# Moving a kernel's operand transposes from TensorE to the DMA queue, with a two-step issue order and a new order of the first chunks

## The chip, the cores and the metric

One core of one Trainium2 chip. The metric is the device time of one execution in microseconds (us). A span in a profile is shorter than the device time of the same execution, mostly by 1.7 to 1.8 us.

The granted clock is the clock that TensorE got, as a share of full speed (1.00). The DMA share is the mean busy share of the core's 16 DMA engines, by the time that packets took.

Engines: PE is TensorE's matmul side, PEld its weight load, DVE VectorE, ACT ScalarE, POOL GpSimd, SP SyncE; "SPq" is SP's sequencer. In the traces it issues all loads, stores and DMA transposes of this kernel, one after another (in that of before 99.47 us for 0.36 us, 99.88 for 0.43, 100.40 for 0.65).

## The reference, cut to what matters

```python
def _attn_ref(q, k, v, alpha):                 # (4, 8, 768, 48) each
    for t in range(S):
        state = alpha[:, :, t, :, None] * state + einsum('bhd,bhe->bhde', k[:, :, t], v[:, :, t])
        y[:, :, t] = einsum('bhd,bhde->bhe', q[:, :, t], state)

def _moe_ref(x, w_in, w_out):                  # x (3072, 384), w_in (384, 2048), w_out (2048, 384)
    h = x @ w_in
    return (h * np.cos(h)) @ w_out
```

A gated linear attention with a recurrent state, followed by a feed-forward layer with a cosine gate. The kernel works through the 3072 tokens in 24 chunks of 128.

## The kernel before

Each chunk passes through units that are named by a letter. An order string says in which order the units of all chunks are recorded, and the traces show the engines running their shares in that order: in that of the changed kernel TensorE does F, S, A, G, V, Y, C from 82.07 to 87.87 us and SP v, a, D, k, k, a, D, e, v, e from 69.50 to 82.79 us, as in its string below. The program has no other scheduler. The units that matter here:

```python
    def operands(j, qeng):            # "o": k and q scaled, in bf16, on GpSimd
        nc.gpsimd.tensor_tensor(out=khb[:, j % 3, :, 0:D], in0=k_sb, in1=icp..., op=ALU.mult)
        qeng.tensor_tensor(out=qhb[:, j % 3, :, 0:D], in0=q_sb, in1=cp..., op=ALU.mult)
        # [cut: v cast, decay of the state]

    def transposes(j):                # "T": eight 128x128 transposes on TensorE, into PSUM
        t = ps.tile([C, 2 * NP * C], BF, tag="g")
        for i, src in enumerate((khb, qhb)):
            for p in range(NP):
                nc.tensor.transpose(t[...], src[:, j % 3, 2 * p : 2 * p + 2]..., ident_bf)

    def ev_transposes(j):             # "t": VectorE copies them to SBUF
        t = work.tile([C, 2 * NP * C], BF, tag="qkT", bufs=3)
        nc.vector.tensor_copy(out=t, in_=qkT_ps.pop(j))

    # "A" scores: 8 matmuls on qkT; "m" mask; "S" state, "u" its update; "Y" outputs, "y" their copy
    # "F","G": halves of ff1, 24 matmuls each; "f","g": cosine on ScalarE; "p","q": gate on VectorE
    # "V","W": halves of ff2, 8 matmuls each; "e": result to SBUF and its store, issued by SP
    # "a","k","v": loads (k stands for k and q); "l","C","E": logarithm, cumulative sum, exponential
    # "w": warm-up matmuls on zeros

    START = ("a0 v0 z0 k0 20 N0 i0 v1 a2 w20 w20 w6 c0 d0 O0 a1 a3 w9 S0 u0 T0 t0 ... "
             "F0 E1 11 21 G0 k3 u1 o2 T2 f0 m1 g0 t2 p0 Y1 y1 A2 ...")        # [cut]
    run(START)
    for s in range(S0, NCH + 2):      # one chunk per step; S0 = 4
        g = (s + 3) // 2
        odd = s % 2 == 1
        V = s - 2 if s - 2 > 1 else -1
        run(f"a{s + 7} k{s + 4} v{s + 4}")
        run(f"o{s + 2} T{s + 1} t{s + 1} F{s} f{s} S{s + 1} u{s + 1} A{s + 1} m{s + 1}")
        run(f"V{V} G{s} g{s} p{s} Y{s + 1} y{s + 1} q{s}")
        if odd:
            run(f"N{g} l{g + 1}")
        run(f"W{V} e{V}")
        if odd:
            run(f"C{g} E{g}")
```

## Time and profile before

| | before |
|---|---|
| device time, median | 208.5 us (207.56 to 209.18, 4 runs) |
| profiled span | 208.2 us |
| PE busy | 196.8 us, 95% |
| PE busy from 70 to 170 us | 100.00 of 100.00 us |
| DMA share from 70 to 170 us | 0.66 |
| chain per two chunks | 14.76 us |

The page's line of busy time, and the lines, from its costliest groups, for the mask that evicts the scores and for the PSUM copy of the transposes. Columns of a group: line, engine, operation, output<-input, shape, count; then busy us and mean ns of one; then the engine's idle time just before.

```profile
PE 196.8 (95%) x2645; PEld 149.0 (72%) x2647; DVE 136.7 (66%) x163; ACT 130.4 (63%) x142; POOL 79.6 (38%) x124
...
L236 DVE TENSOR_TENSOR t<-t,mask_f 128x1024 bf16<-128x1024 f32 x24 | 29.2, 1215 | 0.0
...
L216 DVE COPY t<-t 128x1024 bf16<-128x1024 bf16 x24 | 16.5, 687 | 8.1 <-PE t L210 8.1
```

The table of windows of before. Columns: window in us, its length, busy time of PE, PEld, DVE, ACT and POOL (instructions started), granted TensorE clock, DMA share, GB/s.

```profile
32.00:34.00 2.00, 1.89 (x23) 1.62 (x20) 2.00 (x3) 0.62 (x1) 0.00 (x0) 0.50 0.98 363
...
70.00:170.00 100.00, 100.00 (x1474) 79.89 (x1472) 70.13 (x83) 68.19 (x75) 45.38 (x68) 1.00 0.66 134
```

In the steady part PE is never idle, and VectorE, ScalarE and GpSimd are each busy 71% of the time or less.

The chain of waits of before, in order of time (start us, length us, what). It is PE and nothing else. One period of two chunks runs from one cumulative sum to the next; the pieces on line 210 are the eight transposes of a chunk.

```profile
68.56 0.18 PE cum_new L161
68.74 0.08 PE cum_new L165 x4
68.82 0.47 PE t L210 x8
69.29 1.34 PE t L323 x24
...
75.96 0.45 PE t L210 x8
...
83.32 0.18 PE cum_new L161
```

From 68.56 to 83.32 us is 14.76 us, and 0.47 + 0.45 = 0.92 us of it are transposes. The loop's first ff1 starts at 54.75 us and the last piece of the chain, the last ScalarE copy, at 204.40 us, so the loop takes 149.65 us between these two marks.

### The profile page before, as it was taken

To read this page: it belongs to the slowest core of one execution; us is meant where nothing else is said; L and a number is where in the kernel's file an instruction comes from. 1 tells how busy PE (TensorE), PEld (TensorE's weight loads), DVE (VectorE), ACT (ScalarE), POOL (GpSimd) and SP (SyncE) were. 2 spreads that over 40 slices of the span, in tenths; PEclk is the share of its full clock that TensorE was granted. 3 is DMA by queue.
4 is the path that set the end of the run, shared out by engine and by line. 5 is a ranking of instruction groups with operands and counts; after the bars stand their busy time and mean duration, and the time that the engine had idled before them with its cause. 6 is when DMAs were issued, how large, how long until landed. Compare 5 with 4: busy or idle time off the path is not lost.

```text
span 208.2 us, 6187 instructions
## 1 busy us (share of the span) xinstructions
PE 196.8 (95%) x2645; PEld 149.0 (72%) x2647; DVE 136.7 (66%) x163; ACT 130.4 (63%) x142; POOL 79.6 (38%) x124
## 2 busy tenths in 40 slices
PE   7996869899999999999999999999999999999982
PEld 2343558677787887877878787787878878787851
DVE  7106857799776668487686685766776776777320
ACT  2064594998964955955937839739659558434420
POOL 3005362485570371561730931912804617401000
PEclk9999997999999999999999999999999999999999
DMA  6999999999999377566765955874774461101112
GB/s 139 312 197 319 186 218 360 260 179 199 179 225 191 80 151 157 113 148 123 160 131 93 188 117 106 162 152 97 135 154 94 100 114 43 41 2 39 38 38 77
DMA packets 106204, 30.29 MB, mean 145 GB/s; under 512 B 100288, under 2 KB 105408, under 8 KB 106176
## 3 DMA queue, kind: packets, MB, share of 16 engines
q1 hardware_dynamic: 106176, 29.89, 66.6%
q8 instruction: 20, 0.33, 0.7%
q14 instruction: 8, 0.07, 0.1%
HBM read 25.17 MB, written 4.72 MB: 144 GB/s over the span
## 4 chain that ended last, share of the span: by engine, by line
PE 82%; DVE 6%; DMA 4%; issue 4%; POOL 1%; SPq 1%; ACT 0%; POOLq 0%; DVEq 0%; ACTq 0%
PE o_new L347 32%; PE t L323 29%; PE t L304 8%; PE t L210 5%; DMA t<-in_k_dram 4%; PE t L227 3%; PE t L249 2%; PE cum_new L161 1%; DVE w_114 L121 1%; DVE g_new L338 1%; DVE t L216 1%; DVE qhb L193 1%; PE cum_new L165 1%; DVE t L309 1%; DVE t L236 1%
## 5 line engine op out<-in xcount | busy, mean ns | idle before, releaser
L331 ACT ACTIVATE c_sb<-t,halfpi 128x1024 bf16<-128x1024 f32 x48 | 53.3, 1115 | 41.7 <-PE t L323 41.3
L323 PE MATMUL t<-t,w_114 128*128 128x128 bf16 x1152 | 72.6, 220 | 0.4 <-DVE g_new L338 0.4
L347 PE MATMUL o_new<-w_116,g_new 128*128 128x384 bf16 x384 | 70.2, 327 | 0.6 <-ACT o_sb L363 0.6
L323 PEld LDWEIGHTS <-w_114 128*128 128x128 bf16 x1152 | 67.9, 99 | 3.5 <-issue 0.5
L338 DVE TENSOR_TENSOR g_new<-t,c_sb 128x1024 bf16<-128x1024 f32 x48 | 58.4, 1219 | 15.2 <-ACT c_sb L331 14.7
L191 POOL TENSOR_TENSOR khb<-t,icp_new 128x384 bf16<-128x384 f32 x24 | 25.0, 1041 | 74.8 <-ACT icp_new L179 73.7
L347 PEld LDWEIGHTS <-g_new 128*128 128x128 bf16 x384 | 34.1, 98 | 24.2 <-issue 0.8
L263 POOL TENSOR_TENSOR ub<-sc,Em 128x384 bf16<-128x384 f32 x20 | 17.4, 870 | 33.1 <-DVE sc L261 33.1
L236 DVE TENSOR_TENSOR t<-t,mask_f 128x1024 bf16<-128x1024 f32 x24 | 29.2, 1215 | 0.0
L193 POOL TENSOR_TENSOR qhb<-t,cp_new 128x384 bf16<-128x384 f32 x22 | 22.0, 1000 | 0.0
L216 DVE COPY t<-t 128x1024 bf16<-128x1024 bf16 x24 | 16.5, 687 | 8.1 <-PE t L210 8.1
L309 DVE CAST t<-t 128x384 bf16<-128x384 f32 x24 | 13.3, 554 | 11.4 <-PE t L304 11.3
L363 ACT ACTIVATE o_sb<-o_new 128x384 f32<-128x384 f32 x22 | 10.7, 485 | 15.9 <-PE o_new L347 15.8
L261 DVE TENSOR_TENSOR sc<-t,ub 128x384 f32<-128x384 f32 x20 | 11.1, 557 | 13.8 <-PE t L249 13.8
L370 PE MATMUL w_ps<-warm 128*128 128x512 bf16 x61 | 17.3, 435 | 1.4 <-DVE warm L56 1.2
L331 ACT ACT_TABLE_LOAD x13 | 16.7, 1283 | 0.2
L141 ACT ACT_TABLE_LOAD x13 | 16.7, 1283 | 0.2
L304 PE MATMUL t<-t,vpb 128*64 128x128 bf16 x288 | 15.9, 222 | 0.2 <-DVE t L216 0.2
L179 ACT ACTIVATE icp_new<-cum_new 128x768 f32<-128x768 f32 (+1 forms) x13 | 9.8, 757 | 7.3 <-PE cum_new L165 7.3
L370 PEld LDWEIGHTS <-warm 128*128 128x128 bf16 x63 | 6.5, 109 | 10.4 <-issue 4.5
L304 PE MATMUL t<-t,ub 128*64 128x128 bf16 x160 | 13.0, 227 | 1.0 <-DVE t L216 0.8
L304 PEld LDWEIGHTS <-vpb 128*64 128x64 bf16 x288 | 13.1, 111 | 0.9 <-issue 0.4
(47 smaller groups left out, 152.9 us busy)
## 6 DMA issues: line engine op xcount, KB each, us to landing
a_new<-in_alpha_dram SPq DMA_DIRECT2D x24, 192.0 KB, 3.7
t<-in_v_dram SPq DMA_DIRECT2D x24, 192.0 KB, 4.3
t<-in_k_dram SPq DMA_DIRECT2D x24, 192.0 KB, 4.0
t<-in_q_dram SPq DMA_DIRECT2D x24, 192.0 KB, 4.3
out_dram<-o_sb SPq DMA_DIRECT2D x24, 192.0 KB, 2.0
w1f<-in_moe_w_in_dram SPq DMA_DIRECT2D x2, 1536.0 KB, 7.8
w2f<-in_moe_w_out_dram SPq DMA_DIRECT2D x2, 1536.0 KB, 10.3
```

Of the source, the lines that this page charges most:

```text
L141: nc.scalar.preload_act_table_set("natural_log_exp_and_others")
L191: nc.gpsimd.tensor_tensor(out=khb[:, j % 3, :, 0:D], in0=k_sb, in1=icp.rearrange("s (h d) -> s h d", h=H), op=ALU.mult)
L193: qeng.tensor_tensor(out=qhb[:, j % 3, :, 0:D], in0=q_sb, in1=cp[:, 0:HD].rearrange("s (h d) -> s h d", h=H), op=ALU.mult)
L216: nc.vector.tensor_copy(out=t, in_=qkT_ps.pop(j))
L236: nc.vector.tensor_tensor(out=t.rearrange("s (h t) -> s h t", h=H), in0=A_ps.pop(j).rearrange("s (h t) -> s h t", h=H), in1=mask_f.unsquee ...
L263: eng.tensor_tensor(out=ub[:, j % 3, :, 0:96].rearrange("r p (a e) -> r p a e", a=2), in0=sc.rearrange("r p (a e) -> r p a e", a=2), in1=E ...
L304: nc.tensor.matmul(t[64 * half : 64 * half + 64, kt * C : (kt + 1) * C], lhsT, rhs, start=start, stop=stop, skip_group_check=True)
L323: nc.tensor.matmul(t[:, f], w1[:, kk, ft * C : (ft + 1) * C], x_t[j][:, kk], start=(kk == 0), stop=(kk == 2))
L331: nc.scalar.activation(out=c_sb, in_=h_ps[j, half], func=AF.Sin, bias=halfpi, scale=1.0)
L338: nc.vector.tensor_tensor(out=g_t[j][:, half * HF : (half + 1) * HF], in0=h_ps.pop((j, half)), in1=c_t.pop((j, half)), op=ALU.mult)
L347: nc.tensor.matmul(o_ps[j][:, 0:DM], g_t[j][:, ft], w2[:, ft], start=(f == 0 and (half == 0 or not whole)), stop=(f == HF - 1 and (half == ...
L370: nc.tensor.matmul(w_ps, warm[:, 0:C], warm, start=True, stop=True)
```

## The change

Its intent: from chunk 8 on, the eight transposes leave TensorE and become one DMA transpose (unit "D"), SBUF to SBUF, of 128x1024 bf16 elements. k and q share one tile so that one DMA does both. The loop now records two chunks per step, in an order that was searched in a timing model and that places each D, each load and each store. The order of the first chunks was searched likewise.

```diff
+    JT = 8
-    qhb = consts.tile([C, 3, H, 64], BF, tag="qhb")
-    khb = consts.tile([C, 3, H, 64], BF, tag="khb")
+    kqb = consts.tile([C, 3, 2, H, 64], BF, tag="kqb")
     [cut: the same renaming where they are written and read]
+    def dma_transposes(j):
+        t = work.tile([C, 2 * NP * C], BF, tag="qkT", bufs=3)
+        nc.sync.dma_start_transpose(t.rearrange("r (p s) -> r p s", s=C),
+                                    kqb[:, j % 3].rearrange("s i h d -> s (i h d)"))
+        qkT_t[j] = t
     START = (
-        "a0 v0 z0 k0 20 N0 i0 v1 a2 w20 w20 w6 c0 d0 O0 a1 a3 w9 S0 u0 T0 t0 i1 k1 z1 c1 10 d1 k2 "
+        "v0 a0 k2 k0 a1 i1 a2 a4 a3 i0 w20 w20 w7 c0 d0 O0 w7 T0 z0 t0 S0 k1 10 c1 d1 l1 u0 v1 "
     [cut: the rest of both strings]
-    for s in range(S0, NCH + 2):     [cut: the loop of before, shown above]
+    STEPS = (
+        "T1 t1 o2 v4 F0 S1 A1 a8 m1 f0 o3 u1 G0 p0 D2 g0 V-2 Y1 C2 k4 k5 E2 y1 W-2 T2 a9 q0 F1 "
+        "N2 D3 e-2 t2 S2 A2 V-1 m2 l3 f1 u2 v5 G1 g1 Y2 p1 y2 W-1 q1 e-1 "
+    )
+    for s in range(4, NCH + 2, 2):
+        for u in STEPS.split():
+            n = int(u[1:]) + (s // 2 if u[0] in "NlCE" else s)
+            if not (u[0] in "VWe" and n < 2 or u[0] in "Tt" and n >= JT or u[0] == "D" and n < JT):
+                run(f"{u[0]}{n}")
```

In the names of a double step, D2 and D3 transpose chunks s+2 and s+3. A2 reads the first in the same double step, A1 of the next reads the second.

## The prediction

> **What bounds the kernel now.** From about 54 us on, TensorE alone. The page gives PE 95% busy, granted clock 0.99; the table of 10 us windows shows PE 10.00 of 10.00 from 60 to 190 us, with DVE, ACT and POOL below 9. The chain of waits is nothing but PE pieces from 54 to 198 us. Two chunks take 14.76 us (the cumulative sums stand at 68.56, 83.32 and 98.08 us). Each chunk's eight transposes are 0.45 to 0.47 us of that chain. Before 54 us the DMA share is about 1.0, PE's first useful matmul comes at 14.4 us, and the chain passes through loads, casts, operands and PSUM copies.
>
> **What the change does.** For chunks 8 to 23 the 8 PE transposes and DVE's PSUM copy (687 ns each) go: 16 x 0.46 = 7.4 us of PE and 11 us of DVE. Only the PE part lies on the chain. In their place come 16 DMA transposes of 256 KB (SBUF to SBUF) on SP's queue, which also carries the loads.
> [...] From 80 to 170 us the DMA share is 0.65, about 9.6 us per two chunks[...]. Issue on SP: loads take 0.4 to 0.8 us each, about 6 us per two chunks. [...]
> Latency: D2 is issued about 3 us into a double step, two loads ahead of it, and its scores come 4 us later. D3 stands behind five loads, but is read 7 us later. I expect both to land in time, the first with little slack.
> The two-step order keeps PE's amount of work; a PE that never waits gains nothing from it.
> The first-chunks order gives up the early first weight load (11th transfer, not third), takes the weight cast out of ACT's way ahead of the first logarithm, and runs both first ff1 halves before the second weight half is needed. Adding loads up at 1 us each and 4.5 us per weight half (estimates from the GB/s row), PE can be kept busy from about 30 us; the opening ends at 50 to 54 us against 54.3. I count 2 us.
>
> **On the critical path.** 7.4 us (steady) + 2 us (opening) - 0.5 us (late transposes) = about 9 us. Predicted 199.5 us (ratio 0.957), 196 to 204.5 for 8 in 10. Faster by over 2%: 0.80; within 2%: 0.12; slower by over 2%: 0.08.
>
> **What would show it.** PE at 10.00 of 10.00 from 70 to 180 us; 13.8 to 13.9 us per two chunks; transposes landing 2 to 5 us after issue; DMA share 0.75 to 0.9 in the steady part; the loop's first ff1 at 51 to 54 us. Wrong would be: scores waiting for the transposed tile, loads late at POOL, or SP's issues closing up without gaps.
>
> **What would make it wrong.** A DMA transpose that takes more of the engines than its bytes say[...]; an issue on SP of over 4 us; loads queued ahead of a transpose making it late each step; or an opening in which the later weights cost more than the earlier operands give.

The sum of the critical path: 7.4 + 2 - 0.5 is 8.9, about 9 us, and 208.5 - 9 is 199.5 us. The 0.5 us in it is worked out from no trace. The 0.4 to 0.8 us for a load's issue are the usual ones: in the trace of before, from 60 to 172 us, it took 0.65 us in the median, 0.39 to 2.15 us in all, and SP's issues came to 5.0 to 7.7 us per two chunks. The 4 us of issue that would make it wrong is an estimate from the 6 and 13.8 us: two of them would fill what is left.

## More of the kernel before

The profiled execution is one draw among the runs: that of before took 209.99 us, more than any of the four timed ones.

## The result, and the profile after

| | before | after |
|---|---|---|
| device time, median | 208.5 us (4 runs) | 202.9 us (202.03 to 203.05, 4 runs) |
| ratio | | 0.9726 (95% interval 0.9679 to 0.9772) |
| profiled span | 208.2 us | 200.3 us |
| chain per two chunks | 14.76 us | 13.87 us |
| loop, first ff1 to last copy | 149.65 us | 142.50 us |
| DMA share from 70 to 170 us | 0.66 | 1.04 |

A ratio is the mean time of one kernel's fast runs over that of the other's of the same rounds, so it is not quite the ratio of the medians quoted.

The same two windows of the changed kernel:

```profile
32.00:34.00 2.00, 2.00 (x39) 2.00 (x37) 0.73 (x2) 1.79 (x3) 0.00 (x0) 1.00 1.11 338
...
70.00:170.00 100.00, 100.00 (x1456) 77.89 (x1451) 66.71 (x73) 72.22 (x78) 46.99 (x71) 1.00 1.04 176
```

One period of its chain of waits, where no piece of the transposes' line is left:

```profile
73.63 0.27 PE cum_new L161
...
74.24 1.32 PE o_new L353 x8
75.56 1.34 PE t L329 x24
76.90 0.17 PE t L255 x4
77.07 0.33 PE t L233 x8
...
87.50 0.27 PE cum_new L161
```

And the transposes in its table of DMA issues (count, then median us from issue to landing):

```profile
t<-kqb SPq DMA_TRANSPOSE x16, 4.1
```

87.50 - 73.63 is 13.87 us. The chain goes on without a break: PE is still at 100.00 of 100.00 us, and no score matmul (line 233) waits for a DMA anywhere in the run. The first ff1 of the loop starts at 53.83 us and the last copy at 196.33 us, 142.50 us: 7.15 us less than before. The profile shows 7.9 us of gain, the timed runs only 5.6. The experiments had to explain that difference, and what each of the three parts of the change contributes.

### The profile page after: what moved, and what is told of

The parts are those of the page before. It is cut to its first block, busy times and chain, and to the rows that moved or that the text cites. A ratio compares the mean times of both kernels' runs of the same rounds, so it can differ in the third digit from the quotient of the medians.

```text
span 200.3 us, 5940 instructions
## 1 busy us (share of the span) xinstructions
PE 190.6 (95%) x2535; PEld 141.0 (70%) x2535; DVE 126.0 (63%) x146; ACT 126.5 (63%) x139; POOL 78.1 (39%) x124
## 3 DMA queue, kind: packets, MB, share of 16 engines
q1 hardware_dynamic: 123072, 34.09, 90.8%
## 4 chain that ended last, share of the span: by engine, by line
PE 82%; DVE 7%; issue 5%; DMA 2%; SPq 1%; POOL 1%; ACT 0%; POOLq 0%; DVEq 0%; ACTq 0%
PE t L329 31%; PE o_new L353 31%; PE t L310 7%; PE t L233 3%; DMA t<-in_k_dram 2%; DVE g_new L344 2%; PE t L210 2%; PE cum_new L161 2%; PE w_ps L376 2%; PE t L255 2%; DVE t L242 1%; DVE t L216 1%; DVE t L315 1%; PE cum_new L165 1%; SPq L105 1%
## 5 line engine op out<-in xcount | busy, mean ns | idle before, releaser
L329 PE MATMUL t<-t,w 128*128 128x128 bf16 x1152 | 72.0, 219 | 0.9 <-DVE t L315 0.7
L329 PEld LDWEIGHTS <-w 128*128 128x128 bf16 x1152 | 67.0, 98 | 6.1 <-DVE t L315 0.8
L353 PE MATMUL o_new<-w,g_new 128*128 128x384 bf16 x384 | 69.9, 326 | 0.7 <-ACT o_sb L369 0.6
L191 POOL TENSOR_TENSOR kqb<-t,icp_new 128x384 bf16<-128x384 f32 x24 | 24.2, 1010 | 27.3 <-ACT icp_new L179 14.8
L193 POOL TENSOR_TENSOR kqb<-t,cp_new 128x384 bf16<-128x384 f32 x22 | 22.0, 1000 | 1.8 <-DMA t<-in_q_dram 1.8
L376 PE MATMUL w_ps<-warm 128*128 128x512 bf16 x79 | 20.4, 408 | 1.3 <-DVE warm L58 1.2
L195 POOL CAST vpb<-t 128x384 bf16<-128x384 f32 x24 | 12.5, 520 | 19.6 <-DMA t<-in_v_dram 12.7
L148 ACT ACTIVATE lnab<-a_new 128x768 bf16<-128x768 f32 (+1 forms) x13 | 10.2, 798 | 10.3 <-DMA a_new<-in_alpha_dram 8.2
L376 PEld LDWEIGHTS <-warm 128*128 128x128 bf16 x79 | 7.7, 104 | 10.9 <-issue 3.1
L310 PE MATMUL t<-t,ub 128*64 128x128 bf16 x160 | 12.9, 225 | 0.9 <-DVE t L216 0.8
L310 PEld LDWEIGHTS <-ub 128*64 128x64 bf16 x160 | 9.8, 109 | 5.4 <-issue 2.9
```

The source lines that it names most:

```text
L191: nc.gpsimd.tensor_tensor(out=kqb[:, j % 3, 0, :, 0:D], in0=k_sb, in1=icp.rearrange("s (h d) -> s h d", h=H), op=ALU.mult)
L193: qeng.tensor_tensor(out=kqb[:, j % 3, 1, :, 0:D], in0=q_sb, in1=cp[:, 0:HD].rearrange("s (h d) -> s h d", h=H), op=ALU.mult)
L310: nc.tensor.matmul(t[64 * half : 64 * half + 64, kt * C : (kt + 1) * C], lhsT, rhs, start=start, stop=stop, skip_group_check=True)
L329: nc.tensor.matmul(t[:, f], w1[:, kk, ft * C : (ft + 1) * C], x_t[j][:, kk], start=(kk == 0), stop=(kk == 2))
L353: nc.tensor.matmul(o_ps[j][:, 0:DM], g_t[j][:, ft], w2[:, ft], start=(f == 0 and (half == 0 or not whole)), stop=(f == HF - 1 and (half == ...
L376: nc.tensor.matmul(w_ps, warm[:, 0:C], warm, start=True, stop=True)
```

## The experiments

Eleven runs in three batches, each batch on one chip together with the kernel before. Where a later text says "the loop", it means the stretch from its first ff1 to the last copy.

| run | what it is | median us | ratio to before |
|---|---|---|---|
| e0_after, e10_after | the changed kernel again | 202.92, 202.2 | 0.972, 0.9687 |
| e1_no_dma | both new orders, all transposes on TensorE | 209.45 | 1.0051 |
| e2_old_start | the changed loop, the old first-chunks order | 202.64 | 0.9705 |
| e3_dma_only | DMA transposes in the old orders, behind the step's loads | 208.78 | 1.0035 |
| e4_dma_late | the same, in the step that reads them | 330.17 | 1.5798 |
| e5_dma_first | as e3, but ahead of the step's loads | 204.03 | 0.975 |
| e6_start_warm | as e2, with 7 more warm-up matmuls | 201.58 | 0.9646 |
| e7_from6 | as e6, DMA transposes from chunk 6 | 204.45 | 0.9785 |
| e8_from7 | as e6, DMA transposes from chunk 7 | 202.02 | 0.9675 |
| e9_twice | as e6, every DMA transpose issued twice | 210.06 | 1.0058 |

### The changed kernel again (e0_after)

No edit.

> The changed kernel once more, as it is, so that the parts can be compared with it on the same chip. Both theories: 202 to 203.5 us, ratio to the kernel before 0.969 to 0.977.

202.92 us, ratio 0.972: the first measurement holds. The profile of this run, with a clock of 1.0, has these two marks, the loop's first ff1 and the last copy:

```profile
54.86 1.34 PE t L329 x24
...
197.36 0.49 ACT o_sb L369
```

The loop is 142.50 us again, but it starts at 54.86 us, 1.03 us later than in the first profile of the changed kernel (53.83), and no earlier than in that of before (54.75).

### The two orders without the DMA transposes (e1_no_dma)

```diff
-    JT = 8
+    JT = 24
```

> The changed kernel with all 24 chunks transposed on TensorE: the two new orders alone, no DMA transpose. Theory (only the 16 chunks' transposes on TensorE's chain are worth anything in the steady part): 7.0 to 7.4 us longer than the changed kernel, so 209.5 to 210.5 us, ratio to before about 1.007. Rival (the two-step order is what gains, by ending waits): at most 2 us longer, 203 to 205 us. Period per two chunks: theory 14.76 us.

209.45 us, ratio 1.0051 (interval 1.0017 to 1.0086), 6.5 us longer than the changed kernel. The theory asked for 7.0 to 7.4 us: the medians fall 0.5 us short of that, while the interval covers the ratio given, 1.007. The rival (at most 2 us) fell. The chain of waits of this run has these two marks, the loop's first ff1 (21 of its 24 matmuls lie in the queried window) and the last copy:

```profile
53.85 1.17 PE t L329 x21
...
203.50 0.49 ACT o_sb L369
```

203.50 - 53.85 is 149.65 us, the loop of before to the hundredth. So for a TensorE that never waits the two-step order is worth nothing in the loop. The two new orders together made the kernel slower, by the mean about 1 us, and with equal loops that can only be the opening.

### The old order of the first chunks (e2_old_start)

```diff
     START = (
-        "v0 a0 k2 k0 a1 i1 a2 a4 a3 i0 w20 w20 w7 c0 d0 O0 w7 T0 z0 t0 S0 k1 10 c1 d1 l1 u0 v1 "
+        "a0 v0 z0 k0 20 N0 i0 v1 a2 w20 w20 w6 c0 d0 O0 a1 a3 w9 S0 u0 T0 t0 i1 k1 z1 c1 10 d1 k2 "
     [cut: the whole string of before, with a11 added at its end]
```

> The changed kernel's loop and DMA transposes behind the first-chunks order of the kernel before. The measured gain is 5.6 us, and the loop alone shows 7.0 us in the two traces. Theory (the new first-chunks order costs over a us in most runs, and the profiled run of before was a slow draw): 200.5 to 202 us, at least 1 us shorter than the changed kernel. Rival (the new first-chunks order is worth its 1 to 2 us, as the two traces show): 204 us or more, at least 1 us longer.

202.64 us (201.11 to 202.72), 0.3 us shorter than the changed kernel in the same batch. Neither side is met: the new opening brings nothing, but it doesn't cost over 1 us either, in the median. The single runs tell more. The old opening has more than one kind of run. With a granted clock of 1.0 this kernel's span was 199.2 us (one run), with 0.989 to 0.996 it was 200.5 to 200.9. The kernel before shows the like over the three batches: 10 of its 33 runs had a clock of 0.999 or more and spans of 205.7 to 206.2 us, 23 had 0.99 to 0.992 and 206.9 to 208.3 us, 1.4 us more by the means. Like compared with like in this batch, the spans of this run are 6.5 us (lower clock) and 6.8 us (full clock) shorter than those of before, near the loop's 7.15. The window of before from 32 to 34 us, shown above, is the fall of the clock: 0.50. The window of this run's table for the same time:

```profile
32.00:34.00 2.00, 1.89 (x23) 1.62 (x20) 2.00 (x3) 0.49 (x1) 0.00 (x0) 0.50 1.05 385
```

The windows of before give 0.72 from 30 to 32 us, 0.50 to 34 us, 0.85 to 35 us and 1.00 after that. Ahead of the fall, from 28 to 30 us, TensorE was busy for 0.81 of 2.00 us at a clock of 1.00, and the longest gap between matmuls that the trace shows from 14 to 36 us was 0.78 us. What brings the fall on, and why some runs of one kernel have it and others not, these windows don't show.

The two profiles show 7.9 us where the timed runs show 5.6, because they are draws from opposite ends. The profiled execution of before took 1.5 us more than the median of its timed runs (209.99 against 208.5), that of the changed kernel 0.9 us less (202.03 against 202.9). The fall of the clock alone doesn't explain this. Most timed runs of before have the lower clock too, and they form two groups themselves: 17 with spans of 206.9 to 207.5 us and 6 with 208.0 to 208.3, where the profile stands. And in the changed kernel's sixteen runs it is the longer ones that have the full clock: 201.0 to 201.3 us at 1.0, 199.9 to 200.6 at 0.995 to 0.999. What else differs between runs was not found.

The new opening mostly avoids the fall (0.995 or more in all sixteen runs of the changed kernel), yet ends no earlier: the loop starts at 54.86 us in e0_after and at 54.67 in e10_after. The chain of waits of the changed kernel's first profile has warm-up matmuls on it, 4.2 us in all. That of before has none. The new order string has 79 of them, the old one 63:

```profile
17.94 1.75 PE w_ps L376 x8
...
20.62 1.19 PE w_ps L376 x5
...
22.26 1.29 PE w_ps L376 x6
```

Just before the loop it passes through DVE:

```profile
49.28 0.56 DVE o_sb L367
...
50.36 1.21 DVE t L242
51.57 1.13 DVE g_new L344
52.70 0.47 DVE t L315
```

Yet TensorE is busy for 3.41 of the 3.90 us from 49.3 to 53.2 us there, so in that stretch these evictions hold it up for no more than about 0.5 us. Neither the warm-up matmuls nor the evictions were tested by a run of their own. Why the new opening ends no earlier stays open.

### The DMA transposes alone (e3_dma_only)

```diff
-        run(f"o{s + 2} T{s + 1} t{s + 1} F{s} f{s} S{s + 1} u{s + 1} A{s + 1} m{s + 1}")
+        T = f"T{s + 1} t{s + 1}" if s + 1 < JT else ""
+        DT = f"D{s + 2}" if s + 2 >= JT else ""
+        run(f"o{s + 2} {DT} {T} F{s} f{s} S{s + 1} u{s + 1} A{s + 1} m{s + 1}")
```

> The kernel before, both its orders kept, with the DMA transposes alone: issued right behind each chunk's operands, one step ahead of the scores, after that step's four loads. Theory (a TensorE that never waits gains nothing from the two-step order, and one step is lead enough): 7.0 to 7.4 us shorter than before, 201 to 202 us, ratio 0.965 to 0.968, period 13.8 to 13.9 us per two chunks. Rival (the two-step pattern is needed to bring the transposes in time past the loads): scores wait each step, ratio above 0.98.

208.78 us, ratio 1.0035 (0.9995 to 1.0074). My theory fell: with the same 7.2 us of work taken off TensorE, nothing was gained. The waits of this run (engine, line, what it waited for; total us, times, longest):

```profile
PEld L233 <- DMA t<-kqb: 5.6, 8, 1.2
...
PE t L233 <- DMA t<-kqb: 4.4, 6, 1.1
```

Half of the 16 chunks' score matmuls now wait for their transposed tile. (The expectations of the next two runs add these two lines up, to 14 times and to 10 us. That was a mistake: weight load and matmul wait for the same tile, so it is at least 5.6 us and 8 times.) SP's issues in one step show where the time goes. Columns: start us, us of the issue, what.

```profile
84.82 0.36 SPq L371 DMA_DIRECT2D out_dram<-o_sb  x1
85.22 0.43 SPq L100 DMA_DIRECT2D a_new<-in_alpha_dram  x1
85.70 0.67 SPq L105 DMA_DIRECT2D t<-in_k_dram  x1
86.42 1.90 SPq L105 DMA_DIRECT2D t<-in_q_dram  x1
88.37 0.78 SPq L110 DMA_DIRECT2D t<-in_v_dram  x1
89.31 1.48 SPq L221 DMA_TRANSPOSE t<-kqb  x1
```

The transpose goes out 4.5 us after the store that opened the step, and lands 3.8 us (the run's median) after that, in the next step, when the scores want it. From the first cumulative sum in that stretch to the eighth the seven periods take 14.78 us each, against 14.70 before. The 16 chunks are eight periods, so the counted waits are 0.7 us per period, of the 0.98 that separate 14.78 from the 13.80 of the changed kernel (the mean of six of its periods); the rest I did not follow.

### The transpose in the step that reads it (e4_dma_late)

```diff
-        run(f"o{s + 2} T{s + 1} t{s + 1} F{s} f{s} S{s + 1} u{s + 1} A{s + 1} m{s + 1}")
+        T = f"T{s + 1} t{s + 1}" if s + 1 < JT else f"D{s + 1}"
+        run(f"o{s + 2} {T} F{s} f{s} S{s + 1} u{s + 1} A{s + 1} m{s + 1}")
```

> The kernel before with both its orders; the DMA transpose stands exactly where the eight TensorE transposes stood, in the step that reads it (no lead at all, and one step earlier in the operands' life). Theory (what decides is when the transpose lands against the scores of its chunk, and in the run with one step of lead it came about 0.6 us too late 14 times of 16): with the operands ready a whole step earlier the transpose waits only for SP, which reaches it after a store and four loads, about 4 us into the step; it lands 4 us later while TensorE wants it about 1.5 us into the step: each step waits 5 to 6 us, 16 x 5.5 less 7.2 gives about +80 us, 280 to 295 us. Rival (latency is not what held the one-step version back, but the 16 DMA engines or SP's issue time are full): about the same as the one-step version, 208 to 212 us, since bytes and issues are the same.

330.17 us. The rival fell: with the same bytes and the same issues the kernel is 121 us slower, so it is the landing time that decides. My number was too small twice over. The waits are longer than 5.5 us:

```profile
PEld L233 <- DMA t<-kqb: 97.2, 16, 7.4
```

And in the stretches with these waits the granted clock is lower: 0.84, 0.60 and 0.74 in the three windows from 150 to 180 us, 0.83 in the mean of the run, against 0.992 in e3. A window of its table:

```profile
160.00:170.00 10.00, 7.46 (x68) 5.24 (x69) 3.42 (x4) 1.11 (x1) 1.75 (x4) 0.60 0.26 42
```

An ff1 half at 165.61 us, shortly after a wait of 7.20 us, takes 2.60 us; the next one, at 170.14 us, takes 1.50. 16 waits make 97 us, which leaves 31 us between 330 and (202 + 97) us. The pages of the runs show most of it: the same 2519 PE instructions kept PE busy for 219.0 us here and for 191.3 us in e3, 27.7 us more, at a mean clock of 0.83 against 0.992.

### The transpose ahead of the loads (e5_dma_first)

```diff
-        run(f"a{s + 7} k{s + 4} v{s + 4}")
-        run(f"o{s + 2} {DT} {T} F{s} ...")
+        run(f"o{s + 2} {DT} a{s + 7} k{s + 4} v{s + 4}")
+        run(f"{T} F{s} ...")
```

> The kernel before with both its orders and one-step lead as in the run that gained nothing, but each transpose is issued ahead of that step's four loads instead of behind them. Theory (the transpose's place in SP's queue decides, not the two-step order): it goes out about 3 us earlier, waits of scores for the transposed tile fall from 10 us to under 2, and the time is 201.5 to 203.5 us, ratio 0.966 to 0.975. Rival (only the two-step order hides it, or the DMA engines are full): ratio above 0.985.

204.03 us (202.23 to 204.69), ratio 0.975. One unit moved past four loads in one queue turns 208.78 into 204.03 us, with both orders of before otherwise kept. The waits:

```profile
PEld L233 <- DMA t<-kqb: 0.5, 1, 0.5
PE t L233 <- DMA t<-kqb: 0.4, 1, 0.4
```

SP's issues in one of its steps:

```profile
100.23 1.24 SPq L221 DMA_TRANSPOSE t<-kqb  x1
101.51 0.57 SPq L100 DMA_DIRECT2D a_new<-in_alpha_dram  x1
102.14 0.62 SPq L105 DMA_DIRECT2D t<-in_k_dram  x1
```

So the two-step pattern is not necessary; a place in the queue that lets the transpose land in time is. The median is 0.5 us outside the range given and 1.4 us longer than that of e2 (an earlier batch), which has the same opening and the two-step loop. So the two-step order keeps a small advantage here. In the profile the loop takes 144.39 us (first ff1 at 53.94, last copy at 198.33) against 142.50, and only 0.5 us of these 1.9 are seen as waits for the transposes; the rest was not followed.

### Warm-up matmuls in the old opening (e6_start_warm)

```diff
-        "... F0 E1 11 21 G0 k3 u1 o2 T2 f0 m1 g0 "
+        "... F0 E1 11 21 G0 k3 u1 o2 w3 T2 w4 f0 m1 g0 "
```

(on top of e2)

> The changed kernel's loop behind the old first-chunks order (the run of it had 201.1 us where the clock stayed at 1.0 and 202.6 us where it fell to half for 3 us at about 31 us), with 3 warm-up matmuls before and 4 after the third chunk's transposes, where TensorE stood nearly idle from 28 to 30.6 us. Theory (the fall of the clock is brought on by that idle stretch, and the old order is the better one without it): clock 1.0 in every run, 200.5 to 201.5 us, ratio 0.961 to 0.966. Rival (the fall of the clock is not brought on by the idle stretch): two populations as before, median 202.6 us.

201.58 us (200.83 to 201.86), ratio 0.9646. The fall of the clock is gone from the stretch around 32 us in the profile (1.00 in every window from 22 to 38 us), but three of the six runs still have a clock of 0.991 to 0.996, so the theory's "1.0 in every run" failed. The times are less spread, and this version has the lowest median of all: its six runs lie below all but one of the changed kernel's sixteen (201.66 to 203.13 us), most of which are from other batches. That is about 1 us, half a per cent. What brings the fall on is left open: in the runs e5 and e7, which have no such fall at 32 us, it stands at 22 to 24 us instead (0.69 and 0.66).

### From chunk 6 on (e7_from6) and from chunk 7 on (e8_from7)

```diff
-    JT = 8
+    JT = 6        # e7_from6
+    JT = 7        # e8_from7
```

(each on top of e6)

> The same as the run with the warm-up matmuls, but with DMA transposes from chunk 6 on instead of 8: two transposes more, in a stretch where the DMA engines' share is still above 1.0. Theory (each transpose taken off TensorE's chain is worth 0.45 us wherever it lands in time): 0.9 us shorter than that run. Rival (with the loads of the first chunks still queued they land late, and scores wait): no shorter, or longer by 1 us or more.

> As the run with the warm-up matmuls (201.6 us), but with DMA transposes from chunk 7 on: one more than in it, one fewer than in the run from chunk 6, whose chunk 6 came 2.8 us late and chunk 7 0.8 us late. Theory (chunk 6 was held up by the first chunks' loads in SP's queue, and chunk 7 mostly by chunk 6): chunk 7 alone lands in time, 201.0 to 201.4 us. Rival (the stretch up to 75 us is as a whole too full for a transpose): no shorter than 201.6, up to 202.5 us.

From chunk 6: 204.45 us, nearly 3 us longer than e6; the rival holds. The waits of that run:

```profile
PEld L233 <- DMA t<-kqb: 4.2, 3, 3.0
```

Chunk 6's transpose is issued at 61.19 us although its operands were ready at 56.6; SP was still busy issuing the loads and stores of the opening, without a gap of over 0.1 us from 55.01 us on. It landed 2.8 us late. From chunk 7: 202.02 us with an interval of 0.9642 to 0.9708, which covers the 0.9646 of e6: the 0.45 us expected can't be seen. The transposes nearly all land in time there (0.3 us of wait), so this run is inconclusive on the gain and shows no loss. In the profile its loop is 0.2 us shorter than that of e6, about the 0.45 less the wait. The change's choice of chunk 8 leaves nothing measurable behind.

### Every DMA transpose twice (e9_twice)

```diff
         nc.sync.dma_start_transpose(t.rearrange("r (p s) -> r p s", s=C), kqb[:, j % 3]...)
         qkT_t[j] = t
+        x = work.tile([C, 2 * NP * C], BF, tag="scrap", bufs=3)
+        nc.sync.dma_start_transpose(x.rearrange("r (p s) -> r p s", s=C), kqb[:, j % 3]...)
```

(on top of e6)

> As the run with the warm-up matmuls, but each DMA transpose is issued twice, the second time into a tile that nobody reads: the same transposes, twice their cost on the DMA engines and on SP. One lone transpose took about 2.5 us times 16 engines by the DMA share[...], and the share in the steady part is 1.05. If the share means that the engines are full (2.5 us each is real), two more per two chunks take the period from 13.87 to about 17 to 19 us, 225 to 245 us. If [...]the share counts waiting, the engines have room and only SP's longer issue (about 13.5 of 13.87 us) can make transposes late: 201.5 to 206 us.

For the 2.5 us, the trace of e3 has a transpose with little beside it, at 180.03 us: the DMA share from 180 to 184 us adds up to 2.94 us, the store issued at 179.56 us included. The 13.5 us of SP's time are the author's estimate; in the changed kernel, with half the transposes, SP's issues took 9.2 to 13.3 us in six periods of 13.87 us.

210.06 us, 8.5 us above e6: between the two. The DMA engines were not full at a share of 1.01, since in the window from 70 to 170 us they now moved 194 GB/s instead of 177 at a share of 1.09. But there is little room: TensorE is down to 92.38 of 100 us, and the waits show two causes, loads that come late (26.7 us in the first line, 7.4 us in e6) and transposes that come late. This kernel has three lines more, so the scores are on line 236:

```profile
POOL vpb L195 <- DMA t<-in_v_dram: 26.7, 9, 4.4
...
PEld L236 <- DMA t<-kqb: 9.0, 7, 2.2
```

The cost of one transpose on the engines follows from the DMA queue's own share of the spans: 69.8% of 207.4 us in e1 (no DMA transposes), 87.2% of 201.3 us in e0 (16), 86.4% of 200.0 us in e6 (16) and 95.9% of 207.3 us in e9 (32). (175.5 - 144.8) / 16 is 1.9 us of all 16 engines each, and (198.8 - 172.8) / 16 is 1.6 us. By the changed kernel's other two profiles against e1 it is 2.3 us (90.8% of 200.3 us) and 1.9 us (e10, 86.8% of 201.1 us). How much of this is packets waiting beside other traffic was not separated.

### The changed kernel a third time (e10_after)

No edit.

> The changed kernel once more, to stand beside the two runs of this batch. Both theories: 202 to 203.5 us, ratio 0.969 to 0.977.

202.2 us, ratio 0.9687, 0.2 us above e8 in the same batch.

## Why the prediction was right, point by point

The range held the result (202.9 in 196 to 204.5) and the direction was right. The point, 199.5, was 3.4 us too low.

- **What bounds the kernel, right.** TensorE alone in the steady part, before and after: 100.00 of 100.00 us both times.
- **7.4 us off TensorE's chain, right.** The loop became 7.15 us shorter (149.65 to 142.50), and e1, with the transposes back on TensorE, has 149.65 us again. All five profiles of the changed loop (first, e0, e2, e6 and e10) have 142.50 us, whatever their opening. VectorE's 11 us (16 x 0.687) lie off the chain.
- **The transposes land in time, right, and in the main for the reasons given.** Issue to landing 3.2 to 5.8 us, median 4.1, no score waits. The scores came 4.9 to 7.2 us after the issue of D2, where 4 was expected, and 5.2 us or more after that of D3, where 7 was: the first has about as much slack as the second. SP's issue took 1.68 us in the median (1.24 to 3.48), and 1.28 us in e5; the prediction's estimate of it rested on a figure that no run shows and is cut. One sign that the prediction called wrong did show: from 70 to 170 us GpSimd waits 12.9 us for loads of v, k and q, and in before not at all. It cost nothing, since PE stayed at 100.00 of 100.00 us.
- **"The two-step order keeps PE's amount of work; a PE that never waits gains nothing from it", half right.** It holds word for word where TensorE transposes (e1). But it passed over what such an order has to do: keep the transposes out from behind the loads. In the old loop, placed carelessly, they gained nothing at all (e3) or cost 121 us (e4); one move in SP's queue brought most of the gain back (e5). The prediction named this danger in its last paragraph and put 0.5 us of late transposes in its sum, but gave the order no part in keeping that number small.
- **DMA cost per transpose, wrong in size.** It was 1.6 to 2.3 us of all engines, and the share went to 1.04, not 0.75 to 0.9. The author's estimate of the cost was lower. It did no harm here, since no score waited, and there was some room left: in e9 even twice the transposes cost 8.5 us, where full engines were expected to cost 23 us or more.
- **"I count 2 us" for the opening, wrong. This is the term that was mis-sized.** It measured -0.3 us (e0 against e2) to about -1 us (e1 against before, with equal loops). The sum is then 7.15 - 1 or so = 6 us, against 5.6, 5.9 and 6.7 us between the medians of the three measurements. The 50 to 54 us given for the loop's first ff1 held in the first profile (53.83), by luck of the draw: in the other two it is 54.86 and 54.67 us. The comparison was wrong as well: 54.75 us before was a slow draw in which the clock had fallen. Without the fall, spans of before are 206.0 us by the mean, 2.2 us shorter than that of its profile, and so about what was counted as the gain.
- **0.5 us for late transposes** was not used.

## What to carry to other kernels

Work moved here from the bounding engine to a queue was worth nearly its whole duration where it landed before its reader (7.15 of 7.4 us of the loop), nothing where half of it landed up to 1.2 us late (e3, 208.78 against 208.82 us), and cost 121 us where all of it came up to 7.4 us late (e4); so find the work's place in the issuing queue, behind which loads and stores, before counting the gain. Before comparing two profiles' openings, look at the span and the granted clock of every timed run: here the runs of one kernel lie in groups over 1 us apart, the clock sorts them for before but not for the changed kernel, and a profile is one draw. Two marks that enclose the loop gave the same length in every profile and so left the draw out. An order found for a model is worth measuring part by part: of the three parts here one gained 7 us, one put it where it could be gained (one move in the old order did most of the same), and one gained nothing.
